# Attention and MLP in one kernel: the loads of the second batch's first keys and queries move ahead of w_in, and the hand-written order of all engines is replaced

## The chip, the cores and the metric

One core of one Trainium2 chip runs the whole program. The metric is the device time of one execution in microseconds; three runs of the kernel before took 257.36, 257.59 and 257.74 us, so the median is 257.59 us. TensorE (PE) does the matrix products, VectorE (DVE), ScalarE (ACT) and GpSimd (POOL) the rest, and SyncE (SP) issues nearly all DMAs. Each engine works through its own list of instructions in order; between engines only semaphores wait.

## What is computed

Causal attention in which each query sees its own block of 64 keys and the best of the gated blocks, and then an MLP with a tanh GELU. Cut to what matters:

```python
batch, n_heads, seq, head_dim = (4, 8, 768, 64)
k_rep = k.reshape(B, H, n_blocks, 64, D).mean(axis=3)
gate_scores = np.einsum('bhsd,bhnd->bhsn', q, k_rep)      # causal blocks only
top_idx = np.argsort(gate_scores, axis=-1)[..., -3:]      # plus the own block
scores = where(mask & causal, 0.125 * q @ k.T, -1e9)
attn_out = softmax(scores) @ v                            # (B, H, S, D)
x = attn_out.transpose(0, 2, 1, 3).reshape(3072, 512)
out = gelu_tanh(x @ w_in) @ w_out                         # w_in 512x2048, w_out 2048x512
```

## The kernel before, in words

**Units of work.** The 4 batches times 8 heads are taken as 16 pairs of heads, p = 0 to 15; pairs 0 to 3 are batch 0, pairs 4 to 7 batch 1, and so on. A batch passes through *prepare* for each pair (load k, q and v; turn k and q so that the head dimension lies on partitions; sum k over blocks; gate; choose blocks; make the mask), then *heads* (scores on PE, exp on ACT, the causal triangle on POOL, the product with v on PE, the division on DVE, a turn of the result into `xT`), then `s1` (x times w_in on PE, GELU on ACT) and `s2` (times w_out on PE, sums and output).

**Batch 0 and the later ones differ.** Pairs 0 to 3 are turned by PE (`turn`, lines 545 and 548) and their attention is `heads2` (scores at line 863, exp at line 882, triangle at line 908, product with v at line 931, division at lines 949 and 950). For pairs 4 to 15 the loads come in pieces of 32 floats (`part`, line 400) into the buffers `sd`, and DVE turns them by one transposition of 128x768 (line 564, `tr`), sums the blocks (line 621, `ks_all`), scales (line 638, `ksb_m`), and k and q are cast to fp16 (line 633, `kc_all`, and line 750, `q16`; the copy itself stands at lines 363, 365 and 367 for ACT, POOL and DVE). The gate is eight matmuls on PE (line 687), DVE takes its result (line 703), chooses blocks (lines 710 to 724, `sel_e`), PE turns the mask of pairs 4 to 7 (line 756, `mask`) and two copies bring it into the queries (line 803, `mc`). Scores of pairs 4 to 15 are line 1046, their exp line 1059, triangle line 1073, product with v line 1085.

**The first MLP.** `s1(0)` is 16 units of eight matmuls (line 1122); a unit j, h reads half 0 of w_in for j below 4 and half 1 from j = 4 on. `s2_plain(0)` is 96 matmuls of 512 columns (line 1322), in which PE's list mixes the scores of batch 1. Both weights are loaded from POOL's queue in two halves each (`load_w`, line 460); that of w_in begins with a small POOL copy that reads the last v of batch 0 (line 458), so that it waits for that load.

**What sets the order.** Every piece of work is an `add(...)` of the plan and gets the next number. Nothing is scheduled at run time: `Plan.run` walks the list `ORDER` and emits operation by operation, on the engine that the operation names or that the table `ENGINE` names instead; `BUFFER` gives the buffer of each. So `ORDER` is the instruction order on every engine. Its numbers from 194 on mean the same in both kernels. The ones that the text uses:

| number before | number after | operation |
|---|---|---|
| 57, 58 | 57, 58 | the two DMAs of v of pair 3, the last v of batch 0 (SP) |
| 149, 151, 153, 155 | 157, 159, 161, 163 | `fill`: eight small DMAs that put the block rows into `kT` (SP, line 520) |
| 157, 163 | 165, 171 | loads of w_in and of w_out (POOL) |
| 169 | 177 | `hold`: one DMA on SP that reads the end of w_in, so that SP waits until w_in is there (line 1567) |
| 170, 171 and 174, 175 | 149, 150 and 153, 154 | k and q of pair 4: one DMA, then three more, each (SP, line 400) |
| 178, 179 and 182 to 191 | the same | v of pair 4; k, q, v of pair 5 |
| 335, 336, 339, 341 | the same | pair 4 on DVE: k turned, block sums, scaling, q turned |
| 337, 338 | the same | pair 4: the two casts of k |
| 342, 343, 344, 347 | the same | pair 4: gate (PE), its pick-up and the choice of blocks (DVE), turn of the mask (PE) |
| 147, 292 | the same | DVE: mask of pair 3 out of PSUM; first division of pair 2 |
| 313 | the same | PE: scores of the fourth unit of pair 3 |
| 352 to 355, 363 to 366, 393 to 396 | the same | `s1(0)`: units j = 0, j = 2, j = 4 for the first half of the tokens |
| 1890 on | 1890 on | `warm`: matmuls on zeros of 256 columns that nothing reads (line 1524) |

Of the kernel before, what the change touches and what calls it, by code (L numbers as in the profile page):

```python
# [21 lines left out]
    6, 0, 4, 2, 1890, 1891, 1892, 1893, 1894, 1895, 1896, 1897, 1898,  # L22
    1899, 1900, 1901, 1902, 1903, 1904, 62, 9, 63, 64, 15, 3, 1, 71, 72,
    12, 1905, 1906, 73, 75, 74, 76, 77, 1907, 1908, 66, 18, 1909, 1910,
    1911, 1912, 1913, 84, 68, 19, 22, 23, 26, 31, 195, 67, 78, 93, 82, 79,
    85, 200, 194, 32, 27, 35, 80, 98, 95, 94, 100, 83, 99, 196, 36, 39,
    40, 101, 197, 30, 105, 89, 91, 44, 86, 87, 102, 205, 90, 201, 206,
    198, 214, 215, 109, 113, 114, 110, 48, 45, 49, 52, 53, 103, 104, 210,
    120, 115, 111, 219, 57, 121, 58, 220, 211, 5, 106, 118, 202, 207, 208,
    107, 119, 203, 234, 235, 122, 249, 224, 250, 216, 236, 125, 251, 43,  # L30
    212, 240, 129, 133, 229, 217, 123, 124, 126, 131, 221, 241, 130, 230,
    245, 127, 138, 140, 151, 149, 155, 135, 153, 246, 141, 222, 139, 268,
    231, 269, 263, 232, 242, 56, 157, 225, 142, 238, 264, 243, 143, 144,
    265, 270, 254, 145, 247, 255, 134, 252, 61, 283, 279, 226, 256, 237,
    146, 284, 280, 274, 227, 147, 275, 259, 258, 266, 302, 303, 272, 271,
    297, 276, 285, 298, 277, 281, 286, 288, 292, 289, 1914, 308, 309, 304,
    299, 317, 318, 290, 293, 300, 260, 305, 163, 169, 326, 306, 313, 314,
    310, 1915, 322, 261, 328, 294, 311, 295, 323, 319, 315, 320, 324, 363,
    364, 329, 356, 327, 365, 358, 366, 330, 359, 367, 360, 361, 352, 353,
    354, 355, 331, 362, 357, 408, 409, 410, 411, 373, 170, 374, 412, 375,  # L40
    376, 377, 403, 404, 405, 406, 388, 389, 390, 407, 391, 393, 392, 394,
    395, 396, 418, 397, 419, 420, 421, 422, 433, 368, 369, 370, 434, 371,
    435, 436, 437, 398, 399, 400, 401, 372, 378, 438, 439, 379, 402, 380,
    383, 381, 382, 440, 1916, 1917, 1918, 1919, 1920, 441, 384, 385, 386,
    428, 429, 430, 431, 387, 432, 171, 174, 175, 178, 442, 443, 444, 445,
    446, 413, 447, 448, 414, 451, 179, 182, 183, 186, 335, 187, 336, 190,
    452, 453, 339, 415, 423, 338, 341, 454, 1921, 1922, 1923, 342, 337,
    416, 455, 424, 456, 343, 344, 346, 425, 449, 584, 426, 417, 457, 458,
    459, 345, 427, 460, 347, 461, 462, 463, 464, 465, 466, 470, 471, 472,
    349, 566, 473, 348, 561, 587, 334, 585, 588, 474, 553, 475, 590, 567,  # L50
    467, 595, 562, 1924, 591, 594, 570, 568, 569, 476, 592, 477, 478, 593,
    479, 480, 481, 482, 571, 574, 483, 450, 191, 631, 596, 484, 575, 632,
    635, 644, 598, 645, 636, 639, 552, 554, 650, 485, 597, 486, 488, 572,
    573, 489, 490, 491, 557, 492, 493, 618, 648, 555, 556, 692, 583, 640,
    586, 655, 654, 696, 693, 558, 700, 701, 697, 619, 957, 651, 494, 559,
    576, 563, 646, 961, 468, 622, 495, 623, 652, 496, 497, 653, 601, 498,
    577, 602, 560, 614, 615, 564, 656, 499, 605, 500, 958, 624, 501, 502,
    503, 705, 657, 665, 643, 578, 606, 507, 508, 565, 579, 661, 658, 509,
    620, 616, 647, 617, 706, 510, 621, 625, 603, 707, 511, 512, 666, 504,
# [1567 lines left out]
```

## Time and profile before

| | |
|---|---|
| median of three runs | 257.59 us |
| profiled execution: span from first to last instruction | 256.0 us |
| what lies around the span (median less span) | 1.6 us |
| granted TensorE clock, mean | 1.000 |
| busy, share of the span | PE 96%, DVE 75%, ACT 69%, POOL 33% |
| moved by DMA | 32.62 MB, 127 GB/s over the span |

The page gives no time of its own for the profiled execution beside its span; the median of the runs stands 1.6 us above the span. In the timeline a row is: start and length in us from the span's start, engine, line, operation, what it writes and reads, how many; in brackets the idle time of the engine before it and what ended it. "SPq" marks DMA issues: their length is the time for which SP was held by issuing, not the transfer. A matmul's busy time contains its way through a pipeline, so PE's spacing from one start to the next is what it costs. The row of windows gives, for a stretch, each engine's busy time and (x) its instructions, then the granted clock, the mean busy share of the DMA engines (over 1 where several packets are in flight) and GB/s.

### The profile page before, as it was taken

The numbers are of one execution on the slowest core, as the hardware profiler recorded it, in microseconds if no ns is written. First come the engines' busy times: TensorE is split into PE (matmuls) and PEld (weight loads), VectorE is DVE, ScalarE is ACT, GpSimd is POOL, SyncE is SP. The second block draws the span as 40 slices with busy tenths as digits, with TensorE's granted clock in tenths as the row PEclk, the third lists the DMA queues.
The fourth block names the chain that finished last, engine by engine and source line by source line (L and its number), as shares of the span: only waits on it lengthen the run. The fifth ranks groups of instructions, "written<-read, shape, count | busy, mean of one in ns | idle before, by whom it ended". The sixth has DMA issues, their size and how long they took to land.

```text
span 256.0 us, 6451 instructions
## 1 busy us (share of the span) xinstructions
PE 246.5 (96%) x2485; PEld 171.2 (67%) x2485; DVE 191.4 (75%) x539; ACT 176.4 (69%) x225; POOL 84.3 (33%) x163
## 2 busy tenths in 40 slices
PE   7889999999998999999899999999999999999994
PEld 5667686555554566555578888555777786766883
DVE  2769751041989889989999999699889665579954
ACT  2399997634898998667969884566889957557300
POOL 8465970000239366223053853100056620000000
PEclk9999999999999999999999999999999999999999
DMA  8997599999989995999899699532112520040024
GB/s 164 218 208 166 94 212 191 213 161 157 184 142 165 153 143 99 172 179 199 127 174 110 144 188 166 118 94 69 26 34 72 64 74 1 3 165 0 3 82 164
DMA packets 130927, 32.62 MB, mean 127 GB/s; under 512 B 124528, under 2 KB 126928, under 8 KB 130896
## 3 DMA queue, kind: packets, MB, share of 16 engines
q1 hardware_dynamic: 126160, 27.62, 65.4%
q0 software_dynamic: 3136, 4.19, 9.7%
q10 hardware_dynamic: 1600, 0.39, 0.8%
q8 instruction: 19, 0.31, 0.5%
q14 instruction: 12, 0.10, 0.1%
HBM read 27.26 MB, written 6.29 MB: 131 GB/s over the span
## 4 chain that ended last, share of the span: by engine, by line
PE 51%; DVE 16%; SPq 11%; DMA 10%; POOL 4%; issue 3%; ACT 3%; ACTq 1%; DVEq 0%; POOLq 0%
PE bank L1372 17%; PE wide L1122 10%; SPq L400 9%; PE wide L1046 6%; PE wide L1211 5%; DMA w_in<-in_moe_w_in_dram 5%; PE bank L1085 5%; PE bank L1322 3%; DVE qT L367 3%; DMA sd<-in_k_dram 3%; DVE sel L719 2%; DVE s L564 2%; DVE XS L1309 2%; DMA G<-in_q_dram 2%; ACT ats L882 1%
## 5 line engine op out<-in xcount | busy, mean ns | idle before, releaser
L1122 PE MATMUL wide<-xT,w_in 128*128 128x384 f16 x416 | 72.6, 326 | 0.0
L1059 ACT ACTIVATE ats<-wide 128x896 f16<-128x896 f32 x72 | 63.4, 915 | 8.9 <-PE wide L1046 6.2
L1134 ACT ACTIVATE G<-wide 128x768 f16<-128x768 f32 x52 | 42.1, 810 | 27.3 <-PE wide L1122 27.0
L1122 PEld LDWEIGHTS <-w_in 128*128 128x128 f16 x416 | 40.0, 98 | 26.8 <-issue 1.3
L1073 POOL TENSOR_SCALAR_AFFINE_SELECT ats<-ats 128x256 f16<-128x256 f16 x72 | 33.3, 475 | 60.3 <-ACT ats L1059 60.2
L1046 PE MATMUL wide<-qT,kT 76*128 76x512 f16 (+3 forms) x192 | 39.1, 305 | 0.1
L564 DVE STREAM_TRANSPOSE s<-sd 128x768 f32<-128x768 f32 x24 | 23.1, 968 | 18.7 <-DMA sd<-in_k_dram 17.2
L1372 PE MATMUL bank<-w_out,G 128*128 128x256 f16 x216 | 31.4, 272 | 0.0
L1372 PEld LDWEIGHTS <-G 128*128 128x128 f16 x288 | 26.9, 98 | 6.0 <-issue 0.3
L1322 PE MATMUL bank<-w_out,G 128*128 128x512 f16 x96 | 28.1, 379 | 0.0
L365 POOL CAST kT<-s 64x768 f16<-64x768 f32 x17 | 15.2, 891 | 37.5 <-DVE s L564 37.0
L1421 DVE TENSOR_TENSOR osb<-bank,osb 128x512 f32<-128x512 f32 (+1 forms) x38 | 22.1, 592 | 5.1 <-PE bank L1372 4.5
L1085 PEld LDWEIGHTS <-ats 128*128 128x128 f16 x504 | 22.2, 98 | 3.9 <-POOL ats L1073 0.4
L1085 PE MATMUL bank<-v,ats 128*128 128x65 f16 x504 | 24.4, 194 | 0.2 <-POOL ats L1073 0.2
L1046 PEld LDWEIGHTS <-kT 76*128 76x128 f16 x192 | 17.3, 98 | 10.5 <-issue 0.8
L1372 PEld LDWEIGHTS <-XS 128*128 128x128 f16 x216 | 20.0, 98 | 5.5 <-DVE XS L1309 1.5
L1372 PE MATMUL bank<-TS,XS 128*128 128x256 f16 x144 | 22.0, 272 | 0.8 <-DVE XS L1309 0.7
L882 ACT ACTIVATE ats<-wide 128x1024 f16<-128x1024 f32 (+3 forms) x24 | 20.8, 924 | 1.3 <-PE wide L863 0.8
L365 POOL CAST v<-vsd 128x768 f16<-128x768 f32 x13 | 11.4, 875 | 13.8 <-DMA vsd<-in_v_dram 8.8
L969 DVE TENSOR_TENSOR xn<-bank,zr 128x384 f16<-128x384 f32 x24 | 13.4, 558 | 0.8
L719 DVE MAX8 sel<-sel 128x8 f32<-128x12 f32 x160 | 13.2, 158 | 0.6
L1322 PEld LDWEIGHTS <-G 128*128 128x128 f16 x96 | 8.9, 98 | 6.1 <-issue 0.3
(120 smaller groups left out, 358.6 us busy)
## 6 DMA issues: line engine op xcount, KB each, us to landing
out_dram<-osb SPq DMA_DIRECT2D x23, 256.0 KB
vsd<-in_v_dram SPq DMA_DIRECT2D x26, 192.0 KB
sd<-in_k_dram SPq DMA_DIRECT2D x48, 96.0 KB
sd<-in_q_dram SPq DMA_DIRECT2D x48, 96.0 KB
w_in<-in_moe_w_in_dram POOLq DMA_DIRECT2D x2, 1024.0 KB, 11.5
w_out<-in_moe_w_out_dram POOLq DMA_DIRECT2D x2, 1024.0 KB, 14.5
G<-in_k_dram SPq DMA_DIRECT2D x4, 192.0 KB
G<-in_q_dram SPq DMA_DIRECT2D x4, 192.0 KB
```

The costliest lines, as they stand in the source:

```text
L365: nc.gpsimd.tensor_copy(out=out, in_=in_)
L400: nc.sync.dma_start(out=T[key, p][64 * hh + 32 * a:64 * hh + 32 * a + 32], in_=SRC[key][b, 2 * hp + hh].rearrange("(t i) (a j) -> a i t j" ...
L564: nc.vector.transpose(out=T[key + "T32", p], in_=T[key, p].rearrange("p t j -> p (t j)"))
L882: nc.scalar.activation(out=T["at", u][:, :, 0:n], in_=plan.buf[("st",) + u].rearrange("p (h w) -> p h w", h=2)[:, :, 0:n], func=AF.Exp, bi ...
L1046: nc.tensor.matmul(st[:, x:e], kT16[i][h][0:76, s0:s0 + 128], qT16[i][h][0:76, s0 + (x - cb):s0 + (e - cb)], start=True, stop=True)
L1059: nc.scalar.activation(out=T["at", u][:, 0:n], in_=plan.buf[("st",) + u][:, 0:n], func=AF.Exp, bias=0.0, scale=SCALE)
L1073: nc.gpsimd.affine_select(out=dg, in_=dg, compare_op=ALU.is_ge, fill=0.0, base=0, pattern=[[0, 2], [1, 128]], channel_multiplier=-1)
L1085: nc.tensor.matmul(pvv[:, qc, 0:65], at[:, cb + (qc - jc) * 128: cb + (qc - jc + 1) * 128], v16[i][:, jc, h, :], start=(gi == 0 and jc == ...
L1122: nc.tensor.matmul(hps[:, 512 * e:512 * e + HALF], w_in16[:, ci, (2 * j + e) * 128: (2 * j + e + 1) * 128], T["xT", b][:, ci, HALF * h:HAL ...
L1134: nc.scalar.activation(out=G[:, :, h, j, :], in_=plan.buf["hps", b, j, h].rearrange("p (e w) -> p e w", e=2)[:, :, 0:HALF], func=AF.Gelu_a ...
L1322: nc.tensor.matmul(plan.buf["ops", b, ti], G[:, f % 2, 2 * ti // NC, f // 2, ti % (NC // 2) * 128:ti % (NC // 2) * 128 + 128], w_out16[:, ...
L1372: nc.tensor.matmul(dst[:, HD * h:HD * h + HD], FACT[m][0][:, j, t * 128:(t + 1) * 128], FACT[m][1][:, j, :], start=(clear and j == 0), sto ...
```

## The change

The eight DMAs of k and q of pair 4 are issued on SP right behind the last v of batch 0, ahead of the eight `fill` DMAs; `fill` now comes behind them. Both weights keep their place on POOL's queue behind that last v, and `hold` stays behind `fill`; behind `hold` come v of pair 4 and then pair 5. The lists `ORDER`, `BUFFER` and `ENGINE` are replaced as wholes. `ENGINE` moves work between engines: of pair 4 both casts of k go from DVE to POOL, one cast of q and one mask copy from ACT to DVE; of the pairs 7 and 11 to 15 seven casts of k go from POOL to DVE; some dozen other copies change between ACT and DVE in either direction. `NWARM` goes from 72 to 30, and `ORDER` holds 30 `warm` matmuls where it held 39: 26 of the 39 stood ahead of the first matmul of `s1(0)` in PE's list and 13 behind it; of the 30 the last stands behind the first two matmuls of `s1(0)` and the products of pair 3 with v, and none later.

```diff
 ORDER = [
...
-    297, 276, 285, 298, 277, 281, 286, 288, 292, 289, 1914, 308, 309, 304,
...
+    235, 127, 203, 249, 138, 56, 140, 245, 224, 134, 150, 236, 250, 135,
+    141, 232, 237, 139, 251, 258, 268, 246, 269, 238, 142, 243, 263, 279,
+    153, 264, 165, 143, 154, 270, 280, 144, 265, 1918, 226, 335, 247, 283,
+    145, 146, 284, 266, 252, 256, 288, 147, 274, 289, 259, 297, 336, 337,
+    61, 275, 285, 271, 260, 276, 298, 272, 302, 277, 317, 299, 163, 281,
+    157, 339, 341, 286, 292, 290, 227, 300, 303, 304, 305, 322, 318, 161,
+    293, 308, 338, 342, 323, 313, 306, 309, 314, 310, 326, 319, 159, 261,
+    328, 294, 352, 311, 356, 329, 315, 320, 177, 324, 1919, 295, 343, 363,
+    364, 353, 344, 365, 366, 354, 367, 171, 347, 355, 327, 357, 330, 393,
+    394, 345, 346, 395, 396, 178, 408, 179, 182, 183, 397, 409, 410, 411,
...
 BUFFER = [
...
 ENGINE = {
     "ACT": [
...
     "POOL": [
-        586, 587, 646, 647, 707, 972, 973, 1035, 1036, 1097, 1098,
-        1159, 1160, 1425, 1489, 1551, 1612]}
+        337, 338, 586, 587, 646, 647, 972, 973, 1035, 1036, 1097, 1098,
+        1160, 1550, 1613]}
...
-    NWARM = 72
+    NWARM = 30
...
-    prev = ("v", 3)
-    early_4 = True
-    chain = [issued[prev]]
-    moved_w = []
-    for x in ('in', 'out', ('k', HP + 0), ('q', HP + 0), ('v', HP + 0), ('k', HP + 1), ('q', HP + 1), ('v', HP + 1)):
-        if x in weights:
-            dst, src, parts, prio = weights[x]
-            if not fills:
-                fills = [fill(i, chain) for i in range(NB)]
-            load_w(x, dst, src, parts, [ld[prev]] if x == "in" else
-                   [after_w["in", 0]], prio, prev)
-            moved_w = [after_w[x]]
-            chain += moved_w
-        else:
-            if x == ("k", HP):
-                def hold(_):
-                    nc.sync.dma_start(out=after_in[0:1],
-                                      in_=w_in16[0:1, 3, DFF - 16:DFF])
-                chain.append(add({SP: 0.57}, hold, [w_ready["in", 1]] + fills, 40))
-            load(x[1], x[0], chain + (fills if x[1] > HP or not early_4 else []))
-            prev = x
-            chain = [issued[prev]] + moved_w
+    load(HP, "k", [issued["v", 3]])
+    load(HP, "q", [issued["k", HP]])
+    fills = [fill(i, [issued["q", HP]]) for i in range(NB)]
+    load_w("in", *weights["in"][:3], [ld["v", 3]], weights["in"][3], ("v", 3))
+    load_w("out", *weights["out"][:3], [after_w["in", 0]], weights["out"][3],
+           ("v", 3))
+
+    def hold(_):
+        nc.sync.dma_start(out=after_in[0:1],
+                          in_=w_in16[0:1, 3, DFF - 16:DFF])
+    held = add({SP: 0.57}, hold, [w_ready["in", 1]] + fills, 40)
+    moved_w = [after_w["out"]]
+    chain = [held] + moved_w
+    for x in (("v", HP), ("k", HP + 1), ("q", HP + 1), ("v", HP + 1)):
+        load(x[1], x[0], chain)
+        chain = [issued[x]] + moved_w
```

307 rows, old and new, of tables (BUFFER, ENGINE, ORDER) are left out of this document.

## The prediction

> **What bounds the kernel now.** I read the windows first, a stretch per stage: batch 0's attention up to 38.4 us, its first MLP up to 70, the mixture of attention and MLP up to 160, the rest up to the last matmul.
>
> ```profile
> 0.00:38.40 38.40, 34.61 (x526) 25.87 (x527) 25.09 (x115) 27.39 (x40) 26.32 (x62) 1.00 1.00 177
> 38.40:70.00 31.60, 31.60 (x202) 18.03 (x199) 10.63 (x28) 19.40 (x27) 1.65 (x2) 1.00 1.22 182
> 70.00:160.00 90.00, 87.84 (x919) 59.55 (x918) 84.20 (x223) 72.04 (x91) 41.12 (x71) 1.00 1.05 154
> 160.00:252.70 92.70, 92.42 (x847) 67.71 (x844) 71.08 (x173) 57.54 (x69) 15.16 (x28) 1.00 0.25 63
> ```
>
> The first number behind the stretch's length is PE: from 38.4 us on it lacks 0, 2.16 and 0.28 us, 2.4 in all. PE does its list without pause, so only three things can shorten this part: matmuls that go, matmuls that move ahead of 38.4, and those 2.4 us. DVE is nearly as full between 70 and 160 (84.20 of 90), yet idle for two thirds of 38.4 to 70. Where that idle time lies, the timeline of DVE tells:
>
> ```profile
> 29.56 0.53 DVE L724 SCALAR_TENSOR_TENSOR madd<-sel,ownm 128x120 f16<-128x120 f32 x1
> ...
> 35.34 0.20 DVE L949 RECIPROCAL zr<-bank 128x6 f32<-128x6 f32 x1 [2.07 <-PE bank L931]
> ...
> 54.40 0.98 DVE L564 STREAM_TRANSPOSE s<-sd 128x768 f32<-128x768 f32 x1 [14.96 <-DMA sd<-in_k_dram]
> 55.41 0.95 DVE L621 TENSOR_REDUCE ks<-s 128x12 f32<-128x768 f32 x1
> ...
> 57.34 0.98 DVE L564 STREAM_TRANSPOSE s<-sd 128x768 f32<-128x768 f32 x1 [0.18 <-DMA sd<-in_q_dram]
> ...
> 63.94 0.35 DVE L703 STREAM_TRANSPOSE sel<-bank 128x160 f32<-128x160 f32 x1 [5.19 <-PE bank L687]
> ```
>
> DVE waits 14.96 us for the keys of pair 4. That wait is the one that the change removes, and by itself it is worth nothing: PE was full meanwhile. What it is worth is read where PE waits for DVE later.
>
> ```profile
> PE bank L756 <- DVE madd L724: 1.2, 1, 1.2
> PE bank L1372 <- DVE XS L1309: 0.7, 1, 0.7
> ```
>
> These are PE's waits from 38.4 us on, the two large ones: the mask of pair 7 (PE stands before 81.74) and batch 1's sums (before 126.71).
>
> **The loads, step by step.** SP's queue, POOL's loads, the sizes on the page, then the DMA engines in windows:
>
> ```profile
> 19.93 1.47 SPq L394 DMA_DIRECT2D vsd<-in_v_dram  x2
> 21.51 6.26 SPq L520 DMA_DIRECT2D kT<-G  x8
> 41.60 0.58 SPq L1567 DMA_DIRECT2D after_in<-w_in  x1
> 42.22 7.13 SPq L400 DMA_DIRECT2D sd<-in_k_dram  x4
> 49.40 4.83 SPq L400 DMA_DIRECT2D sd<-in_q_dram  x4
> ...
> 55.43 3.07 SPq L400 DMA_DIRECT2D sd<-in_k_dram  x4
> ```
> ```profile
> 26.97 1.66 POOL L460 DMA_DIRECT2D w_in<-in_moe_w_in_dram  x2
> ...
> 34.74 1.78 POOL L460 DMA_DIRECT2D w_out<-in_moe_w_out_dram  x2
> ```
> ```profile
> sd<-in_k_dram SPq DMA_DIRECT2D x48, 96.0 KB
> ```
> ```profile
> 24.00:28.00 4.00, 3.77 (x76) 2.85 (x72) 2.57 (x8) 4.00 (x6) 3.00 (x7) 1.00 0.13 28
> 28.00:30.00 2.00, 2.00 (x44) 1.62 (x40) 1.85 (x12) 1.60 (x4) 1.94 (x4) 1.00 0.67 63
> 30.00:36.00 6.00, 5.91 (x121) 4.58 (x118) 3.64 (x11) 5.37 (x8) 4.79 (x8) 1.00 1.11 210
> ```
>
> The last column shows a hole: from 24 us, when batch 0 has arrived, to 28 the DMA engines move 28 GB/s. In the change SP reaches the eight DMAs when it reached `fill`, at 21.5. Without w_out beside them four took 3.07 us, so 0.77 each: eight are issued by 27.7. From the end of the four issues to the data it took at most 5.1 us beside w_out (k: 49.35 to 54.40) and 3.1 as that transfer ended (q: 54.23 to 57.34). With 3.1, k is there at 27.7 and q at 30.8; with 5.1, at 29.7 and 32.8. DVE wants k after the choice for pair 3, at 30.1 (row 29.56), and q, behind a mask copy, a division, the sums and the scaling, some 3.5 us later. Both are in time, k by 0.4 to 2.4 us. The new wait counts nothing, then; were k later, behind it in DVE's list would stand the mask copy of pair 3 (147) and the divisions of pairs 1 and 2, and behind these PE's scores of pair 3 and ACT's exps.
>
> The eight `fill` DMAs move behind, to 27.7 to 34; the first scores that need them come after 60. `hold` still waits for w_in, at 41.6. Behind it two DMAs of v and then k of pair 5 take the places of k and q of pair 4: the sixth place was issued at about 52.2, so k of pair 5 lands near 57, where DVE took it at 66.02 before. Each later load comes some 6 to 10 us earlier, as far as buffers are free.
>
> **Is w_in late?** Its halves land 9.4 and 13.7 us after their issues (26.97 and 27.89): 36.4 and 41.55.
>
> ```profile
> DMA to landing us min/median/max: 9.4/11.5/13.7
> ```
> ```profile
> 37.56 1.05 PE L931 MATMUL bank<-v,ats 128*128 128x65 f16 x26
> 38.45 1.79 PE L1122 MATMUL wide<-xT,w_in 128*128 128x384 f16 x10
> 40.07 0.33 PE L988 MATMUL bank<-ident,xn 128*128 128x128 f16 x3
> ```
>
> Half 0 has 2 us to spare. Half 1 was first read by the fourth unit; now unit j = 4 (393) comes third. After the last product of pair 3 with v (38.4) PE then has seven pairs of 384 columns, at 0.32 us (five in 38.45 to 40.07), and two turns, 0.5 us at most: it asks at 41.2 or a little before. If what is left of the eight DMAs at 28.5 delays w_in by 0 to 1 us, PE stands 0.3 to 1.4 us, less what DVE or ACT hold it anyway: I take **+0.2**. Below zero it cannot go, and were w_in wholly behind all eight, it would be 8 x 96 KB at the 210 GB/s of row 30.00, +3.7 us.
>
> [...]
>
> **The change in PE's list.** Rows of the fillers and of pair 4's gate:
>
> ```profile
> 56.27 0.71 PE L1524 MATMUL bank<-XS 128*128 128x256 f16 x5
> 56.81 0.38 PE L1322 MATMUL bank<-w_out,G 128*128 128x512 f16 x1
> ...
> 62.98 0.49 PE L1524 MATMUL bank<-XS 128*128 128x256 f16 x3
> 63.40 0.48 PE L687 MATMUL bank<-s,ksb 128*32 128x160 f32 x8
> 63.81 0.50 PE L1122 MATMUL wide<-xT,w_in 128*128 128x384 f16 x2
> ...
> 68.64 0.55 PE L1046 MATMUL wide<-qT,kT 76*128 76x512 f16 x3
> ...
> 70.05 0.27 PE L1524 MATMUL bank<-XS 128*128 128x256 f16 x1
> ```
>
> - *Nine fillers go* from a stretch in which PE has no pause: five cost 56.81 - 56.27 = 0.54 us, 0.108 each: **-0.98**. Four more stood behind 230 us between matmuls that wait for DVE; there I count nothing (0 to -0.43).
> - *The gate of pair 4* (63.40 to 63.81) moves ahead of 38.4, where PE has 3.8 us of pauses: **-0.41**. Its cover is that pause; were it gone, this would be 0.
> - *The wait before 81.74:* pair 4's turn, sums, second turn, pick-up and choice (0.98 + 0.95 + 0.19 + 0.98, then 2 us) leave the stretch from 54 to 66, and pair 5 starts 9 us earlier. Seven casts of k come to DVE later on, at about 0.6 us (below), 4 us in all; only one of them (pair 7) lies before this point. DVE should be 3 us and more ahead: **-1.20**. Late next is then the copy of that mask, which scores further on wait for.
>
> ```profile
> L367 DVE CAST kT<-s 64x768 f16<-64x768 f32 x7 | 4.1, 587 | 0.1
> ```
>
> - *The wait before 126.71:* the sums run on a DVE that is 94% busy and gets as much new work as it has won by then. Half: **-0.36** (0 to -0.72).
> - *New waits* of a list that is new throughout, in batches 1 to 3: the trace shows none of them, and the bounds are 0 and the 2.4 us that the old list has. Between them I take **+0.9**. The other copies that change between ACT and DVE, and the new buffers, I count at nothing beside it: PE, which has no pause, covers them.
>
> **Batch 0's attention.** Here ACT sets the pace:
>
> ```profile
> 13.78 0.51 ACT L363 CAST XS<-bank 128x384 f16<-128x384 f32 x1
> ...
> 34.82 3.26 ACT L882 ACTIVATE ats<-wide 128x1024 f16<-128x1024 f32 x4 [0.43 <-POOL ats L908]
> ```
>
> Behind the first exp eight such copies become six: up to -1.0 us. Against it, DVE turns, sums and scales pair 4 (3.1 us) ahead of the first division of pair 2 (292); its pauses of 2.07 us (row 35.34) and less hide most, and what is left holds PE before pair 3's products and then ACT: up to +1.0. POOL's two casts of k come ahead of the last triangles, while the issue of w_out (1.78 us) goes behind them. Sum: **+0.1**, bounds -1.0 and +1.0.
>
> **Sum.** -0.98 - 0.41 - 1.20 - 0.36 + 0.9 + 0.1 + 0.2 = -1.75. It is made against the span of 256.0 us; taking the 1.6 us around it as unchanged, the median goes from 257.59 to **255.8 us**.
>
> **Rivals.**
> - *w_in comes late (slower).* The loads ahead of it push both halves, and every microsecond for which PE stands at unit j = 4 is lost, since nothing later has a pause to give back. Price up to 3.7 us, so -1.95 + 3.7 = +1.75: 259.3. It turns the sign when half 1 lands more than 2 us after 41.5. For it: 128-byte pieces move slowly (0.77 us per 96 KB). Against it: the hole of 4 us. 20%.
> - *The time won is spent again (no change).* DVE's 15 us served nobody; new waits take all that the fillers, the gate and pair 7 give: 257.1 to 258.1. For it: 84.20 of 90. 14%.
> - *All goes well.* Both waits and the rest of the 2.4 us vanish, and batch 0 ends 1 us earlier: -0.98 - 0.41 - 2.4 - 1.0 = -4.8, 252.8. The step to there, -3 or more, 13%.
> - *TensorE stays slow longer.*
>
> ```profile
> 1.07 3.34 PE L1524 MATMUL bank<-XS 128*128 128x256 f16 x15 [1.07 <-DVE bmask L292]
> 4.25 0.91 PE L545 MATMUL bank<-identk,G 128*128 128x130 f32 x6
> ```
>
> The first 15 fillers take 0.22 us each, later ones half. Now 12 stand there, ending near 3.7 us, 0.6 before the first turns. If the fast state needs more, the turns at 4.25 take twice: +0.9, 256.7. 4%. [...]
> - *The new list stalls PE in batches 1 to 3 for more than it gives*, above 258.1: 4%.
>
> **How the numbers follow.** The forecast (-0.6 to -3 us) has 45%. 0.2%, about 0.5 us, is what a measurement of this kernel can tell from no change. Faster: 45 + 13 + 4 = 62%; same 14%; slower 20 + 4 = 24%. The range leaves out a tenth at either end: the outer part of "all goes well", and the upper half of late w_in: 253.3 to 258.9.
>
> **What would show it.** Right: line 564 at 30 to 32 us without a wait; no line 1524 behind 42 us; line 687 before 38 us; the first scores at line 1046 well before the 68.6 us of now; PE's wait at line 756 gone. Wrong: PE before `s1`'s third unit idle with w_in named; DVE idle before line 564 at 30 us; line 1122 beginning after 39.5; PE's sum of waits from 38.4 us on above 4 us.

## The result, and the profile after

The changed kernel took 265.94 us (median of four executions, 263.47 to 273.14), the kernel before beside it 257.66 us (four executions, 257.36 to 258.02). The ratio is 1.024, with a 95% interval of 1.0223 to 1.0257: **slower by 2.4%**, against a forecast of 255.8 us. The ratio stands below that of the medians because it is taken over the two fast executions (263.47 and 264.34 us) alone. The profiled execution of the changed kernel is the longest of the four, with a span of 271.4 us against 256.0; a second profile (the run `again`, below) has 264.4 us. Neither of the two shortest executions has a profile, so how their 6 us divide is known only from the runs with one edit below. Lines are eight lower than before: the turn by DVE is now line 556, the product with v line 923, the division line 942, the gate line 679, `s1` line 1114.

The same four windows as in the prediction, of the changed kernel (PE, PEld, DVE, ACT and POOL busy, granted clock, DMA share, GB/s):

```profile
0.00:38.40 38.40, 33.09 (x459) 24.31 (x460) 24.11 (x110) 25.13 (x35) 25.64 (x60) 1.00 1.09 185
38.40:70.00 31.60, 25.59 (x205) 15.90 (x205) 12.95 (x35) 14.82 (x20) 4.92 (x7) 0.84 1.00 151
70.00:160.00 90.00, 84.98 (x797) 53.67 (x796) 73.47 (x205) 67.43 (x85) 31.25 (x54) 0.98 0.99 141
160.00:252.70 92.70, 90.79 (x883) 65.78 (x882) 73.82 (x177) 63.70 (x77) 20.81 (x40) 1.00 0.40 69
```

PE, full from 38.4 to 70 us before, now lacks 6 us there, 5 in the mixture and 1.9 at the end, and the granted clock, 1.00 in every stretch before, is 0.84 and 0.98 on the mean. So there are two places and two kinds of loss, standing still and running slowly. What PE waited for, the four longest waits:

```profile
PE bank L923 <- DVE xn L942: 8.2, 1, 8.2
PE bank L679 <- DVE ksb L630: 3.6, 1, 3.6
PE wide L1114 <- DMA xT<-xn: 1.6, 1, 1.6
PE bank L748 <- DVE xn L961: 1.4, 1, 1.4
```

The two waits that the change was to remove (before: 1.2 at the mask of pair 7, 0.7 at the sums) are gone from the list; these four are new, the last of them at the mask of pair 6.

**The first place, 36 to 49 us.** DVE's two turns of pair 4 and its first division after them:

```profile
31.08 0.96 DVE L556 STREAM_TRANSPOSE s<-sd 128x768 f32<-128x768 f32 x1
...
42.71 0.98 DVE L556 STREAM_TRANSPOSE s<-sd 128x768 f32<-128x768 f32 x1 [8.24 <-DMA kT<-G]
43.61 0.16 DVE L941 RECIPROCAL zr<-bank 128x6 f32<-128x6 f32 x1
```

k is turned at 31.08 without a wait, as forecast. q is turned only at 42.71, after 8.24 us of idle DVE; the division of pair 2 stands behind it. PE's product of v, which needs the bank that this division frees, and ACT's next exp wait with it:

```profile
44.41 0.82 PE L923 MATMUL bank<-v,ats 128*128 128x65 f16 x12 [8.18 <-DVE xn L942]
...
49.11 0.59 PE L1114 MATMUL wide<-xT,w_in 128*128 128x384 f16 x2
```
```profile
45.60 0.38 ACT L874 ACTIVATE ats<-wide 128x256 f16<-128x256 f32 x1 [8.92 <-PE wide L855]
```

`s1` starts at 49.11 instead of 38.45 us: **10.7 us late**, more than the wait, since PE's clock had fallen meanwhile (0.56 on the mean from 38.4 to 50). The name behind the 8.24 us, a DMA of `fill`, is the one that came last by the profile on SP's queue; whether it is the cause is the first question of the experiments.

**The second place, 127 us.** PE stands 3.59 us at the gate of pair 11, and its clock is 0.83 on the mean from 126 to 136 us, another 1.7 us:

```profile
126.74 0.48 PE L679 MATMUL bank<-s,ksb 128*32 128x160 f32 x8
130.81 0.48 PE L679 MATMUL bank<-s,ksb 128*32 128x160 f32 x8 [3.59 <-DVE ksb L630]
```

The account of the 15.4 us between the two spans is rough. 10.7 + 3.6 + 1.7 + 1.6 + 1.4 are 19.0; less the waits that went (1.2 and 0.7), the nine fillers (1.0) and the gate of pair 4 (0.4) it is 15.7. But the changed list begins `s1` ahead of the last 26 products with v (0.8 us), which stood before `s1` in the old list. Counted behind them the first place costs 11.5 us, and the account is 1.1 us too long; what gives that back was not traced.

**The queues.** SP's and POOL's issues answer the loads of the prediction:

```profile
21.52 5.04 SPq L392 DMA_DIRECT2D sd<-in_k_dram  x4
26.60 2.23 SPq L392 DMA_DIRECT2D sd<-in_q_dram  x4
28.94 14.37 SPq L512 DMA_DIRECT2D kT<-G  x8
43.43 0.58 SPq L1551 DMA_DIRECT2D after_in<-w_in  x1
```
```profile
27.41 1.66 POOL L452 DMA_DIRECT2D w_in<-in_moe_w_in_dram  x2
```

The eight are issued by 28.83 us (forecast 27.7; k's four took 5.04 us and q's 2.23, where the forecast had 3.07 for each), w_in is issued at 27.41 (before 26.97), and SP's next DMA behind w_in goes out at 43.43 (before 41.60).

The packets of the two queues, first in the three microseconds ahead of w_in's start, then in the ten behind it (q0 is POOL's queue, q1 is SP's; packets, MB, share of the 16 engines):

```profile
q1 hardware_dynamic: 2801, 0.35, 72.8%
q0 software_dynamic: 12, 0.02, 10.4%
```
```profile
q0 software_dynamic: 964, 1.93, 103.1%
q1 hardware_dynamic: 1018, 0.15, 16.6%
```

This is the key view. From 27 to 30 us SP's queue alone sends 2801 packets, 934 per microsecond. From 31 to 41 us, beside w_in, it sends 1018: 102 per microsecond, against 96 of w_in. **One for one** in this window, but a packet of w_in has 2 KB and one of q 128 bytes (1.93 MB in 964; 0.35 MB in the 2801 of the first window). w_in loses next to nothing (1.93 MB in these ten microseconds, 1.98 of POOL's queue in the kernel before), and what is left of q moves nine times slower.

### The profile page after: what moved, and what is told of

The parts are those of the page before. It is cut to its first block, busy times and chain, and to the rows that moved or that the text cites. A ratio compares the mean times of both kernels' runs of the same rounds, so it can differ in the third digit from the quotient of the medians.

```text
span 271.4 us, 6412 instructions
## 1 busy us (share of the span) xinstructions
PE 249.8 (92%) x2476; PEld 172.7 (64%) x2476; DVE 196.2 (72%) x548; ACT 173.3 (64%) x218; POOL 82.6 (30%) x161
## 4 chain that ended last, share of the span: by engine, by line
PE 65%; SPq 14%; DMA 11%; DVE 6%; issue 2%; POOL 0%; ACT 0%; DVEq 0%; ACTq 0%
PE wide L1114 20%; PE bank L1364 20%; PE wide L1038 8%; SPq L386 7%; DMA sd<-in_q_dram 6%; SPq L392 6%; PE wide L1203 5%; PE bank L1314 4%; PE bank L1077 4%; DMA kT<-G 2%; DMA xT<-xn 2%; PE bank L679 1%; DVE ks L613 1%; DVE s L556 1%; DMA G<-in_q_dram 1%
## 5 line engine op out<-in xcount | busy, mean ns | idle before, releaser
L1114 PE MATMUL wide<-xT,w_in 128*128 128x384 f16 x416 | 76.7, 331 | 1.6 <-DMA xT<-xn 1.6
L1051 ACT ACTIVATE ats<-wide 128x896 f16<-128x896 f32 x72 | 62.7, 916 | 7.2 <-PE wide L1038 3.8
L1114 PEld LDWEIGHTS <-w_in 128*128 128x128 f16 x416 | 40.9, 99 | 28.4 <-issue 3.9
L1065 POOL TENSOR_SCALAR_AFFINE_SELECT ats<-ats 128x256 f16<-128x256 f16 x72 | 32.6, 469 | 79.5 <-ACT ats L1051 79.3
L1364 PE MATMUL bank<-w_out,G 128*128 128x256 f16 x216 | 34.5, 272 | 0.0
L1364 PEld LDWEIGHTS <-G 128*128 128x128 f16 x288 | 27.0, 98 | 6.1
L1314 PE MATMUL bank<-w_out,G 128*128 128x512 f16 x96 | 29.4, 379 | 0.0
L1413 DVE TENSOR_TENSOR osb<-bank,osb 128x512 f32<-128x512 f32 (+1 forms) x38 | 22.3, 593 | 5.8 <-ACT osb L355 2.7
L1077 PEld LDWEIGHTS <-ats 128*128 128x128 f16 x504 | 22.3, 97 | 4.4 <-POOL ats L1065 0.6
L1077 PE MATMUL bank<-v,ats 128*128 128x65 f16 x504 | 24.4, 194 | 0.3 <-POOL ats L1065 0.3
L1364 PE MATMUL bank<-TS,XS 128*128 128x256 f16 x144 | 23.5, 272 | 0.0
L357 POOL CAST kT<-s 64x768 f16<-64x768 f32 x15 | 13.7, 915 | 26.5 <-DVE s L556 26.1
L923 PE MATMUL bank<-v,ats 128*128 128x65 f16 x168 | 8.5, 199 | 8.2 <-DVE xn L942 8.2
## 6 DMA issues: line engine op xcount, KB each, us to landing
out_dram<-osb SPq DMA_DIRECT2D x23, 256.0 KB
```

The costliest lines, as they stand in the source:

```text
L357: nc.gpsimd.tensor_copy(out=out, in_=in_)
L1051: nc.scalar.activation(out=T["at", u][:, 0:n], in_=plan.buf[("st",) + u][:, 0:n], func=AF.Exp, bias=0.0, scale=SCALE)
L1065: nc.gpsimd.affine_select(out=dg, in_=dg, compare_op=ALU.is_ge, fill=0.0, base=0, pattern=[[0, 2], [1, 128]], channel_multiplier=-1)
L1077: nc.tensor.matmul(pvv[:, qc, 0:65], at[:, cb + (qc - jc) * 128: cb + (qc - jc + 1) * 128], v16[i][:, jc, h, :], start=(gi == 0 and jc == ...
L1114: nc.tensor.matmul(hps[:, 512 * e:512 * e + HALF], w_in16[:, ci, (2 * j + e) * 128: (2 * j + e + 1) * 128], T["xT", b][:, ci, HALF * h:HAL ...
L1314: nc.tensor.matmul(plan.buf["ops", b, ti], G[:, f % 2, 2 * ti // NC, f // 2, ti % (NC // 2) * 128:ti % (NC // 2) * 128 + 128], w_out16[:, ...
```

## The experiments

Theory A: the tail of q of pair 4 shares the DMA engines with w_in packet by packet; DVE, in order, stands at q's turn. Theory B: what DVE waits for is `fill`, or the order of SP's queue. Theory C: the new lists lose in batches 1 to 3, whatever the loads do. In the copies of the changed kernel lines stand up to five lower than in the changed kernel, in those of the kernel before 11 lower than before.

**again**: no edit.

> The changed kernel unchanged, once more, for a profile beside those of the next three. Theory A (the tail of q of pair 4 shares the DMA engines packet by packet with w_in, and DVE stands in order at q's turn with the divisions of pair 2 behind it): 262 to 268 us, DVE's turn of q (line 556) begins within 2 us of the landing of w_in's second half (42.4), TensorE then stands 6 to 9 us and its granted clock falls. Theory B (what DVE waits for is the `fill` DMAs, or the order of SP's queue as such): the same time, but the turn of q follows the landing of a `fill`, wherever w_in ends. Theory C (the new list loses in batches 1 to 3): the gap to the kernel before opens behind 60 us; by A at least two thirds of it stand at 50 us.

Measured: 266.18 us (four executions, 261.93 to 266.87). Here q came at 37.30, and PE's wait was 2.8 instead of 8.2 us:

```profile
37.30 0.98 DVE L556 STREAM_TRANSPOSE s<-sd 128x768 f32<-128x768 f32 x1 [2.87 <-DMA sd<-in_q_dram]
```

`s1` began at 42.83, 4.4 us late of 8.4 (264.4 against 256.0); with the 26 products that now stand behind its start it is 5.2. That is half to six tenths, a little short of the two thirds that A asked for, and q was turned at 37.30, not within 2 us of the landing of w_in's second half (near 43.0: issued at 28.1, and `hold`, which waits for it, went out at 43.08). The rest stands at pair 11's gate, at 120 us. So A does not explain all; C has its part, and DVE and SP ahead of that gate show which:

```profile
111.33 0.98 DVE L556 STREAM_TRANSPOSE s<-sd 128x768 f32<-128x768 f32 x1 [3.02 <-DMA sd<-in_k_dram]
```
```profile
95.70 0.60 SPq L392 DMA_DIRECT2D sd<-in_k_dram  x1
101.00 1.34 SPq L985 DMA_TRANSPOSE xT<-xn  x1
...
105.86 2.91 SPq L392 DMA_DIRECT2D sd<-in_k_dram  x4
```

The first of pair 10's four DMAs of k goes out at 95.70. Behind it in SP's list stands a DMA that turns pair 6's output; its input is late, so SP stands for 4.7 us. Then the list has q of pair 10 and other issues, and the other three of k follow only at 105.86 (the fourth in that row is pair 11's). DVE waits 3.02 us for them, and the scaling of pair 11 behind it in DVE's list is what PE waits for. This chain is theory C2.

**w_in_after_q**: w_in is held back until q has landed. Its place in the list (165) moves behind q's last DMAs (154).

```diff
-                nc.gpsimd.tensor_copy(out=x, in_=T[after][96:97, 0, 1, 0:16])
+                nc.gpsimd.tensor_copy(out=x, in_=T["q", HP][96:97, 0, 0:16])
```

> The changed kernel, but the small copy on POOL that holds back w_in reads q of pair 4 instead of v of pair 3, so w_in is issued when q has landed. By A, q alone lands at 30 to 33 us, DVE's turn of q begins there without a wait of 5 us or more, w_in's second half lands at 44 to 48, and TensorE stands 2 to 5 us at the third unit of s1 with w_in named: 257 to 262 us. By B the turn of q stays at 41 to 43 as the `fill` DMAs are still behind it in the same queue, and w_in comes later besides: 264 or more. By C 262 to 266, since the list is the same.

Measured: 266.11 us (263.58 to 268.20), ratio 1.030 (1.0246 to 1.0353). POOL's copy and issue, then DVE's turn of q (line 551 here):

```profile
30.81 0.20 POOL L445 COPY after_in<-sd 1x16 f32<-1x16 f32 x1 [3.59 <-DMA sd<-in_q_dram]
31.35 1.67 POOL L447 DMA_DIRECT2D w_in<-in_moe_w_in_dram  x2 [0.34 <-issue]
```
```profile
36.99 0.98 DVE L551 STREAM_TRANSPOSE s<-sd 128x768 f32<-128x768 f32 x1
```

The last DMA of q had landed at 30.81, the very number of the forecast, with the `fill`s issued from 28.24 on behind it: B falls. DVE's wait at q is gone. But POOL now stands 3.59 us with triangles behind it, PE waits 2.8 us for them, `s1` begins at 43.11, and the 3.7 us at pair 11's gate are still there; so the time, expected at 257 to 262 by A, did not improve. The wait for w_in that A expected at the third unit did not come either.

**before_loads_early**: the kernel before with its own lists; only the loads move.

```diff
 ORDER
-... 138, 140, 151, 149, 155 ...
+... 138, 140, 170, 171, 174, 175, 151, 149, 155 ...
```

> The kernel before with its own lists; only the eight DMAs of k and q of pair 4 move ahead of the four `fill`s. DVE turns q where it did (about 57 us), so nothing waits for its landing at 31 to 43. By A: no loss from sharing alone, 256.8 to 258.2, w_in's second half lands at 42 to 43, TensorE stands 0 to 1 us before the third of its units. By C the same. If the loads as such cost (w_in pushed back by the full 3.7 us), 259 to 261.

Measured: 257.82 us (ten executions, 257.55 to 258.02) against 257.60, ratio 1.0008 (0.9999 to 1.0018). PE's wait for w_in:

```profile
PE wide L1111 <- DMA w_in<-in_moe_w_in_dram: 0.2, 1, 0.2
```

The early loads as such cost 0.2 us, the size of the forecast's term, though the interval holds zero. What costs is that somebody waits for them early. The run shows one thing more. DVE did not leave q's turn at 57 us, where the expectation had it, but took up pair 4 as soon as its own list came to it:

```profile
39.12 0.97 DVE L553 STREAM_TRANSPOSE s<-sd 128x768 f32<-128x768 f32 x1
...
41.91 0.98 DVE L553 STREAM_TRANSPOSE s<-sd 128x768 f32<-128x768 f32 x1
...
64.13 0.35 DVE L692 STREAM_TRANSPOSE sel<-bank 128x160 f32<-128x160 f32 x1 [20.81 <-PE bank L676]
```

The wait of 14.96 us for the keys is gone, and DVE idles 20.81 us before the gate instead, which kept its place in PE's list. PE's 1.2 us at the mask of pair 7 stayed.

**q_turn_later**: the loads of the change stay; pair 4's turn of q and what follows from it go back in the lists.

```diff
 ORDER
-... 339, 341, 286, 292 ... 338, 342, 323 ... 295, 343, 363, 364, 353, 344 ... 347 ... 345, 346 ...
+... 395, 396, 341, 178 ... 331, 342, 398, 399, 343, 344 ... 401, 347, 345, 346 ...
```

> The changed kernel with its loads where they are; only DVE's turn of q of pair 4, the gate, pick-up, choice, casts and mask behind it move back in the lists, behind the third unit of s1. By A: DVE's 8 us wait ahead of the divisions of pair 2 goes, s1 starts at 38 to 40 us, the clock stays at full, and the time is 255.5 to 258.5. By B the same, if nothing else in the lists waits for a `fill`; by C 259 to 264, since all behind 60 us is unchanged.

Measured: 265.37 us (264.57 to 266.36), ratio 1.0316 (1.0294 to 1.0338). By A alone this was to be 255.5 to 258.5, so **A as the sole cause fell here**; it also lies above C's 259 to 264. `s1` did start at 38.67, 4.2 us earlier than in `again`, but the span is only 1.6 us shorter (262.8). PE stood at the gate of pair 11 as long as ever, and the moved chain brought waits of its own: DVE 4.27 us for the late gate of pair 4, PE 0.95 us at that pair's mask. Of the 2.1 us below another 0.9 stand at 8.95 us, in batch 0, as in the kernel before:

```profile
PE bank L674 <- DVE ksb L625: 3.7, 1, 3.7
PE bank L743 <- DVE madd L711: 2.1, 3, 0.9
```

**k10_first**: the changed kernel with pair 10's loads (1083, 1086, 1087) ahead of the transposition (687).

```diff
 ORDER
-... 529, 530, 1082, 686, 687, 1039 ...
+... 529, 530, 1082, 686, 1083, 1086, 1087, 687, 1039 ...
```

> The changed kernel with one edit on SP's queue in batch 1: the last three DMAs of k and the four of q of pair 10 go ahead of the transposition of pair 6's output, which holds SP from 96 to 101 us since its input is late. Theory C2 (TensorE's 3.65 us before the gate of pair 11, and the half clock behind it, come from the late k of pair 10 by way of DVE's list): that wait falls to 0 to 1 us, the clock stays at full there, and the time falls by 3.5 to 5.5 us against the changed kernel's 262 to 266: 257.5 to 261. If DVE itself has too much to do there (its list, not the load): the wait stays above 3 us and the time at 262 to 266. Theory A as the sole cause: no change.

Measured: 260.74 us (258.61 to 265.31), ratio 1.009 (1.0056 to 1.0124): C2 holds, and this is the largest single gain of the study. SP's issues, then PE at the gate:

```profile
92.46 2.58 SPq L387 DMA_DIRECT2D sd<-in_k_dram  x4
95.15 3.45 SPq L387 DMA_DIRECT2D sd<-in_q_dram  x4
98.69 1.33 SPq L980 DMA_TRANSPOSE xT<-xn  x1
```
```profile
118.07 0.48 PE L674 MATMUL bank<-s,ksb 128*32 128x160 f32 x8 [1.92 <-DVE ksb L625]
```

The wait fell from 3.65 to 1.92, not to 0 to 1: DVE still waits 1.89 us for the k of pair 11. In the profiled execution q happened to be in time, and the span was 256.9 us, with the clock at 1.00 throughout. The 7 us between this kernel's executions are then, by A, the luck of q, though not that alone: w_in_after_q, in which q cannot meet w_in, spreads by 4.6 us too, at mean clocks of 0.981 to 0.999, so falls of the clock come and go as well. Four profiles whose code is the same up to 45 us show how that luck is made (rows of SP's issues of k and q, of POOL's issue of w_in, and of DVE's turn of q):

| run | k's four issues take | last q issued | w_in issued | q turned |
|---|---|---|---|---|
| k10_first | 3.96 us | 27.69 | 27.33 | 34.47, no wait |
| again | 4.24 us | 28.05 | 27.20 | 37.30 |
| fill_gate (below) | 4.57 us | 28.27 | 27.25 | 40.20 |
| the changed kernel | 5.04 us | 28.83 | 27.41 | 42.71 |

From `again` to the changed kernel 0.78 us later at the issue became 5.4 us at DVE's turn, a factor of 7; from `again` to fill_gate 0.22 became 2.9, a factor of 13. The packets say 9. Why four issues take 4 us in one execution and 5 in another was not settled.

**both**: the last two edits at once.

> The changed kernel with q's turn later in the lists and with pair 10's loads ahead of the transposition, both at once. By A and C2 together both large waits go: 256.5 to 259.5, so nearly all of the 5 to 8 us is explained by the two, and what is left of it is the smaller waits before the masks (1.4 us at about 82 us) and the transposed output (1.3 us at about 165). If a third cause is hidden in the new list, it stays above 260.

Measured: 262.33 us (261.33 to 264.68), ratio 1.019 (1.0154 to 1.0226), **worse than k10_first alone**, and above the 260 that the expectation set as the sign of a third cause. PE waits 2.7 us at the gate of pair 11 instead of 1.9, and its clock falls there (0.79 on the mean from 120 to 124 us, where k10_first has 1.00). That is not all: two of the six executions kept a mean clock of 1.00 and took 261.33 and 261.46, k10_first at 1.00 and 0.999 took 258.61 and 260.09. The rest stays open; the waits that the moved chain brings (0.95 us at the mask of pair 4) are part of it.

**w_in_a_little_later**: k10_first, and POOL's issue of w_in (165) behind the triangle 270.

```diff
 ORDER
-... 153, 264, 165, 143, 154, 270, 280 ...
+... 153, 264, 143, 154, 270, 165, 280 ...
```

> The changed kernel with pair 10's loads ahead of the transposition (as in the earlier run with that edit, 258.6 to 265.3 from execution to execution), and with POOL's issue of w_in behind one more triangle, about 0.7 us later. By A (what of q is unsent when w_in starts moves one packet for each packet of w_in, some 14 times slower than before): q is then through in most executions, the spread shrinks to 2 us or less and the median falls to 258.3 to 260. If the spread comes from somewhere else it stays at 5 us and more, with the median at 260 to 262.

Measured: 260.32 us (six executions, 259.79 to 262.31), ratio 1.0105 (1.0073 to 1.0137). w_in went out at 29.91, more than meant; from 31 to 41 us SP's queue had 144 packets left (the changed kernel 1018, but the profiled execution of k10_first, with q in time, only 192), and DVE turned q at 34.95 without a wait. The spread shrank from 6.7 us (four executions) to 2.5 (six), the way that A says, if not to the 2 us expected. The factor of 14 in the expectation was the author's estimate and is not in the packets, which give 9 (934 to 102 per microsecond in the changed kernel). The median did not fall, since `s1` now starts at 39.8 and PE waits 1.0 us for a triangle.

**repaired**: that kernel, with the gate of pair 11 (1164) behind 796 and its pick-up and choice (1165, 1166) behind 1104.

> The kernel of the run before this one, with the gate of pair 11 some 2.3 us of matmuls later in TensorE's list and its pick-up and choice behind those of pair 10 in DVE's. By C2 the 1.9 us that were left before that gate go to 0 to 0.5: 1 to 2 us less than the run before this one, 257 to 258.5. If another wait takes the place (the mask copies of pair 11, the transposed output at 158 us): no gain.

Measured: 260.25 us (257.73 to 262.42), ratio 1.0075 (1.0052 to 1.0097): no gain over 260.32 in the median. The gate's wait is gone; in its place PE waits for triangles, a copy of q and the transposed output:

```profile
PE wide L1109 <- DMA xT<-xn: 1.3, 1, 1.3
...
PE bank L1072 <- POOL ats L1060: 1.1, 2, 0.8
...
PE wide L1033 <- DVE qT L354: 0.6, 1, 0.6
```

**fill_gate** and **later_filled**: fillers ahead of the gate of pair 11, 34 in the changed kernel, 22 in w_in_a_little_later. Late work stays as late; only the standing still goes.

```diff
-    NWARM = 30
+    NWARM = 52
 ORDER
-... 551, 1102, 1164, 774 ...
+... 551, 1102, 1920, 1921, ... 1941, 1164, 774 ...
```

> The changed kernel with 34 more of the fillers (0.109 us each, 3.7 us in all) ahead of the gate of pair 11, where TensorE stands for 3.65 us. The gate's start does not move, since it waits for DVE. If the half clock behind that wait comes from TensorE having stood still, it stays at full behind 122 us and the time falls by 1.5 to 2.0 us; if it comes from something else (the load of the whole chip, batch 0), nothing changes.

> The kernel of the run w_in_a_little_later (two of its six executions at a granted clock of 0.993 and 262.3 us, four at 0.998 to 1.0 and 260.2), with 22 fillers (0.109 us each, 2.4 us) ahead of the gate of pair 11, where TensorE stood for 2.1 us. If the half clock comes from standing still there: no execution at 0.993, all at 259.8 to 260.8. If it comes from elsewhere: the 262.3 stays in about a third of them.

Measured: fill_gate 266.99 us (263.22 to 270.93), ratio 1.0282 (1.0228 to 1.0335), not below the changed kernel; q came at 40.20 in the profiled execution and its luck covers the 1.5 to 2 us looked for. later_filled, without that luck, 259.85 us (259.66 to 260.09), ratio 1.0087 (1.0072 to 1.0102). A second set of six gave 260.24 (259.63 to 261.72), one of them at the mean clock 0.993 that two of six had without the fillers; so 1 in 10 against 2 in 6, which leans the expected way and proves little by itself. The windows are plainer. The stretch behind the gate in w_in_a_little_later, then in later_filled:

```profile
120.00:124.00 4.00, 3.08 (x16) 1.35 (x17) 3.93 (x19) 0.83 (x1) 0.00 (x0) 0.63 1.46 160
```
```profile
120.00:124.00 4.00, 4.00 (x34) 2.39 (x32) 3.90 (x21) 1.15 (x3) 0.00 (x0) 1.00 1.51 157
```

The gate starts at 120.92 in the one and at 120.51 in the other, but the clock is 0.63 behind 2.09 us of standing and 1.00 behind 22 fillers. In fill_gate, too, it is 1.00 from 124 to 132 us. All three profiles with the 22 fillers (later_filled, its repeat, cold15) have 1.00 from 116 to 128 us. With the same late work the clock fell where PE stood for 2.09 us (0.63), and not where fillers ran (1.00).

**nine_less**: the kernel before without the fillers 1916 to 1924.

> The kernel before without the nine fillers that stand in its list between 42 and 70 us, all else as it was. My prediction's term: -0.98 us, so 256.6 (256.4 to 256.9). If the matmuls behind them wait for something else anyway: 257.4 to 257.8.

> The kernel before without the nine fillers once more, as the measure for the run with the gates moved up: 256.3 to 257.3.

Measured: 256.86 us (256.29 to 256.91), ratio 0.9962 (0.9950 to 0.9974), and 256.54 us (256.34 to 256.71), ratio 0.9957 (0.9942 to 0.9971). The forecast's -0.98 us came as -0.87 and -1.14. It is the best kernel of the study and beats both.

**old_list_early_turn**: the idea on the old lists. nine_less with the early loads, and pair 4's chain in DVE's idle time (also 346 and 345 behind 392, 347 behind 397, 349 and 348 behind 422).

```diff
 ORDER
-... 355, 331 ... 376, 377, 403 ... 
+... 355, 335, 336, 339, 338, 337, 341, 331 ... 376, 377, 342, 343, 344, 403 ...
```

> The idea of the change without its new lists: the kernel before, without the nine fillers of 42 to 70 us, with the eight DMAs of k and q of pair 4 ahead of the `fill`s, and with pair 4's turns, sums, gate, choice, casts and mask moved up into DVE's idle time of 39 to 54 us (q's turn not before 42 us, when w_in is in). If the idea is sound and only the lists of the change lose: the wait of 1.2 us before the mask of pair 7 (80.6 us) goes too and the time is 255.0 to 256.3, below the 256.9 of the kernel without the nine fillers. If an earlier pair 4 is worth nothing: 256.6 to 257.1. If DVE's or ACT's lists stall elsewhere by it: above 257.3.

Measured: 257.34 us (256.57 to 257.75), ratio 0.9969 (0.9957 to 0.9981); nine_less had 0.9962. Pair 4 is done on DVE by 51 us, and **it is worth nothing**. PE's wait at the mask of pair 7 stays, and DVE's idle time has only moved:

```profile
81.22 0.45 PE L745 MATMUL bank<-ident,madd 128*128 128x128 f16 x5 [1.19 <-DVE madd L713]
```
```profile
70.37 0.35 DVE L692 STREAM_TRANSPOSE sel<-bank 128x160 f32<-128x160 f32 x1 [7.96 <-ACT osb L352]
```

```profile
69.75 0.48 PE L676 MATMUL bank<-s,ksb 128*32 128x160 f32 x8
```

DVE, now early with pair 5 as well, idles 7.96 us before the pick-up of pair 5's gate. The profile names an ACT copy that ended last, but the gate itself stands at 69.75 us in PE's list, in its old place; from there on DVE has the same work in the same time.

**gates_up**: that kernel, with k and q of pair 6 loaded earlier and the gates, choices and masks of pairs 5 and 6 some 5 us up.

> The kernel of the run old_list_early_turn (the idea of the change on the lists of before), with what it lacked: there DVE stood idle for 8 us before 70.4 us, since the gate of pair 5 kept its place in TensorE's list, and the wait of 1.2 us before the mask of pair 7 stayed. Now k and q of pair 6 load ahead of the last v of pair 5, and the gates, choices and masks of pairs 5 and 6 move some 5 us up. If the places of the gates in TensorE's list held that wait: it goes, and the time is 0.8 to 1.3 us below the kernel of nine fillers less run beside it. If DVE has its work in the way later anyhow: the wait stays or moves to another mask, and both agree within 0.3 us.

Measured: 261.87 us (261.37 to 262.97), ratio 1.0171 (1.0146 to 1.0195). Neither expectation came: the wait at the mask of pair 7 went, but PE stands 2.76 us for the copies of pair 5's mask, which now stand behind pair 6's choice in DVE's list and end on ACT at 78.3 us, and the clock falls again (0.78 on the mean from 76 to 80 us, 0.80 from 80 to 84):

```profile
78.35 0.58 PE L1311 MATMUL bank<-w_out,G 128*128 128x512 f16 x1 [2.76 <-ACT qT L352]
```

Whether an early pair 4 pays in lists that are consistent on all engines stays open.

**cold15**: later_filled with 15 fillers at the start.

> The kernel of the run later_filled with three more fillers at its start, 15 as in the kernel before where the change has 12. My fourth rival: with 12 the first six turns of k run at half speed (1.64 us for six in the changed kernel, 0.91 in the kernel before). If that holds batch 0 back, the turns go back to about 0.9 us, s1 starts 0.3 to 0.7 us earlier and the time falls by as much: 259.1 to 259.6. If batch 0 waits for its loads and for ACT anyway, the turns are faster and the time stays at 259.7 to 260.1.

> The kernel of the run later_filled once more as the measure for the run with 15 fillers at the start: 259.6 to 260.1.

Measured: cold15 259.89 us (259.58 to 260.52), later_filled_again 260.24 us (259.63 to 261.72). The six turns took 1.01 us instead of 1.55, and `s1` started at 39.87 against 39.73: nothing reaches the end of batch 0. So the fourth rival was right that fewer fillers leave the first turns slow (1.64 us in the changed kernel, 0.91 in the kernel before), and wrong on the price, which is nothing here.

## Why the prediction was wrong, step by step

- **"Both are in time"**, with "the new wait counts nothing", is the step that failed first. k was (31.08). q was in time in some executions (34.47 in k10_first) and late in others (37.30 to 42.71), and PE then stood 2.8 to 8.2 us. For q the prediction took the longest delay between issue and data that the rows showed, 5.1 us, as the bound beside a weight's transfer. But in the changed kernel that delay was longer: q's last DMA was issued by 28.83, and DVE turned q at 42.71, since what SP's queue had left when w_in started went at 102 packets per microsecond. The rows of the kernel before held it: eight DMAs of 96 KB in pieces of 128 bytes are 6144 packets; at the prediction's own 0.77 us for each DMA they are 6.2 us of work, begun when the first is issued at 22.3, so they end at 28.5 at the earliest, behind w_in's issue at 27. The margin was nothing. And the four issues of k took 4.0 to 5.0 us, not 3.1, those of q 2.2; so the eight ended at 27.7 to 28.8, where the prediction had 27.7. Why k's differ, the runs do not tell.
- **What sharing does to q was not priced.** The prediction asked what the eight DMAs do to w_in (0 to 1 us of delay, 3.7 us at the worst), and left q at 5.1 us at most behind its issue. The kernel before had the slower pace in its trace: from 42 to 49.4 us, in which SP issues k's four DMAs beside w_out, SP's queue sent 656 packets, 89 per microsecond, and from 55.4 to 58.5, beside no weight and with some of v among them, 3386, 1092 per microsecond. In the changed kernel the packets (1018 against 964 of w_in) show both sides: q late, w_in not.
- **Who stands behind it** was named for a late k: pair 3's mask copy, the divisions, PE's products, ACT's exps. It came so, for q; but in the prediction it is an aside without a price or a chance. The rival "w_in comes late", which got the 20%, did not come: PE's waits in the changed kernel do not name w_in, nor do those of k10_first, where `s1` came almost in time, and alone it costs 0.2 us. The rival that the new list stalls PE in batches 1 to 3, with 4%, is the second half of the loss (k10_first).
- **w_in, +0.2:** right in size (before_loads_early), though there half 1 is asked for by the fourth unit; with the changed list and q in time (k10_first) no wait for w_in shows.
- **Nine fillers, -0.98:** right (-0.87 and -1.14).
- **The gate of pair 4, -0.41:** it does stand ahead of `s1` (46.29 in the changed kernel); not tried by itself.
- **The wait before 81.74, -1.20:** wrong as reasoned. The prediction added up DVE's work that moves away, and did not ask what DVE waits for on the way: in the kernel before it had already caught up at 70.87 us, where it waited 0.52 us for PE's gate. old_list_early_turn took all of pair 4 away and the 1.19 us stayed. The seven casts of k that this term and the text on the change name are miscounted: by the two tables six go from POOL to DVE and two (of pairs 14 and 15) come back. With the two of pair 4 that leave, DVE has 9 such casts instead of 7.
- **The wait before 126.71, -0.36:** the sums are no longer among PE's waits; more than forecast, but new waits stand elsewhere.
- **New waits, +0.9, bounds 0 and 2.4:** the upper bound was no bound, for the waits of an old list say nothing about those of a new one. In the changed kernel the waits behind 50 us are 3.6 + 1.6 + 1.4 = 6.6 us, and the half clock adds 1.7. This is the second step that failed: the 3.6 to 3.7 us at the gate of pair 11 stand in every profile of the changed lists in which neither pair 10's loads nor fillers were put ahead, whether q was late or not.
- **The clock** was a term that the sum lacked. Every price of a wait was the wait alone. In the changed kernel the 3.59 us of standing at the gate of pair 11 cost besides half of the 3.4 us at half clock behind them (0.51 on the mean from 131.3 to 134.7 us), in `again` the 3.6 us there half of twice that (122.1 to 129.0, worked out from the means of 0.77, 0.50 and 0.88 in the three windows of 4 us from 120 on).
- **Batch 0, +0.1 (bounds of 1.0):** too small, even where q was in time. `s1` begins at 38.67 (q_turn_later) and 39.10 (k10_first) instead of 38.45, but ahead of 26 products with v that stood before it in the old list:

```profile
39.10 0.49 PE L1109 MATMUL wide<-xT,w_in 128*128 128x384 f16 x2
39.43 0.98 PE L918 MATMUL bank<-v,ats 128*128 128x65 f16 x26
...
43.08 7.64 PE L1109 MATMUL wide<-xT,w_in 128*128 128x384 f16 x46
```

  At 43.08 k10_first has done 16 matmuls of `s1` and three turns; the kernel before had done as much at about 41.2 (10 matmuls by 40.07, the turns, and 6 more from 40.24 on at 0.16 us). Of these 1.9 us the gate, the mask and a filler that now stand ahead are 0.8, so some 1.1 us are lost, at the upper bound.

What is left with the first cause out of the way and the second halved shows in k10_first's profile, the shortest of its four executions: with q in time the span is 256.9 us, 0.9 above the kernel before, with waits of 1.9, 1.4 and 0.4 us behind 50 us where the old list has 2.4 from 38.4 us on. The kernels in which q was safely in time and PE did not stand at that gate (repaired, later_filled) took 260.25 and 259.85 us, still 2 us more than the kernel before. So no form of the changed lists that was run is a gain.

## What to carry to other kernels

What the two queues shared here was not bytes: beside w_in's 96 packets of 2 KB per microsecond SP's queue, with q's pieces of 128 bytes, sent 102, and 934 just before. Count the packets that a transfer of small pieces has left when one of large pieces starts, and divide by a rate that a trace shows beside such a transfer, before you say that it is in time. An engine that runs in order should not be given a load's first reader just behind the earliest landing, when others wait behind it. And a load that is moved ahead of idle time pays only if the instruction that ends the next idle time, on another engine, moves too.

## What the runs showed of the hardware that was not expected

- TensorE's granted clock fell after short pauses: behind 2.09 us of standing (w_in_a_little_later: 0.63 on the mean from 120 to 124 us), 2.7 (both: 0.79 from 120 to 124), 2.76 (gates_up: 0.78 from 76 to 80) and 3.59 (the changed kernel: 0.50 from 131.5 to 134.5), and not behind 1.92 us:

```profile
120.00:124.00 4.00, 4.00 (x27) 2.49 (x26) 3.76 (x29) 3.16 (x4) 0.83 (x1) 1.00 1.32 197
```

  This is k10_first behind its 1.92 us (118.07); it has 1.00 from 116 to 120 and from 124 to 128 us too. The shortest pause with a fall behind it is 2.09 us.
- w_in took no harm from a thousand small packets beside it: 1.93 MB in the ten microseconds from 31 to 41, with 1018 packets of SP's queue, 1.88 MB in k10_first with 192, and 1.98 MB in the kernel before with none.
- A transfer that may miss by a microsecond goes with executions that differ by 7 to 10 us (k10_first, the changed kernel), where those of the kernel before differ by 0.7 to 1.4. The falls of the clock have a part in that, which was not separated.
